# First MoE: the two halves of a tile's transposes set apart, with the next tile's last product piece and its exponential between them

## The chip, the cores and the metric

The program runs on one core of one Trainium2 chip. The metric is the device time of one execution in microseconds; before the change the median of three runs is 1106.28 us.

## The reference

Three stages follow one another. Attention: for 4 batches and 8 heads of 576 tokens and head size 64, scores q·kᵀ/8 plus a position bias from a small two-layer network, softmax, times v. Its output, seen as 2304 tokens of 512 values, is the input of the first MoE block; the output of that is the input of the second. The change is in the first block:

```
h = x @ w_in                                # 2304 x 512 by 512 x 1024
e = exp(h - max(h));  sm = e / (sum(e) + 1e-9)
solu = h * sm
ln = (solu - mean) / sqrt(var + 1e-6) * g_ln
x2 = ln @ w_out                             # 1024 x 512
```

The second block is `(sigmoid(x2 @ w_gate) * (x2 @ w_val)) @ w_out2`, with a width of 1536.

## The kernel before, in words

**Number format.** Every fp32 operand of a product is cut into a high and a low fp16 part, and a product is three fp16 products (high·high, high·low, low·high) summed in PSUM.

**Attention** runs in 72 ticks. In tick t TensorE does the scores of tick t (`a_qk`, s_ps, L500), the products with v of tick t-4 (`a_pv`, xps, L560) and, in some ticks, transposes of finished outputs (`a_xt`, xtp, L606), of q (`prep_q`, qtp, L276) and of k (`prep_k`, ktp, L237). VectorE adds the bias and takes the row maximum (L520), ScalarE takes the exponentials (L525, L527), ScalarE or VectorE and then GpSimd cut the result into fp16 parts (L536 to L540), and a DMA on SP's queue transposes them (pt).

**First MoE.** There are 18 tiles of 128 tokens. For one tile i the steps, in the code's terms, are: `m_g1`, the first product in four pieces, two (half 0, half 1) for each of two column halves n = 0, 1, of 6 matmuls of 512 columns each (L702, into hps); after half 1 of each n VectorE copies the accumulator out and takes its maximum (L713). `m_ew1`: the exponential on ScalarE (e, L723) and the product with h on VectorE (L727). `m_ew2`: squares on ScalarE (L733), the power on GpSimd, then the normalisation on GpSimd (L738). `m_ew3`: the layer transposes, two halves of four fp32 transposes each (ltp, L747); each half is copied out as the fp16 high part by ScalarE (lt, L749), and VectorE subtracts for the low part (L750). `m_g2`: the second product in four pieces dc of 24 small matmuls (x2ps, L761); a piece reads all eight 128-column blocks of lt, the four of the first half first. With dc = 3 the result is copied out (L766, L767) and stored (x2_d, L769).

**What sets the order.** A generator, `moe_items`, lists these steps. For each i it gives the four pieces of `m_g1(i)`, then `m_ew1(i)`, then `m_ew3(i-1)` with both halves, then `m_ew2(i)`, then the four pieces of `m_g2(i-1)`: eleven items a tile. From the moment the bias work is over, each tick takes three items (NB = 3), after `a_qk` and ahead of `a_pv` and `a_xt`. The transposes of q and k that a tick brings come right behind the first of the three items. A tile's first piece has to wait for its tokens, so that some ticks take no item. In the attention stage TensorE's order is the written one (`manual_schedule`); that of the other engines is made by the planner, from priorities and modelled times, attention ahead of MoE. hps, ltp, x2ps, qtp, ktp and xtp share three PSUM buffers (`ps_m`); hps of one n holds its buffer from half 0 until VectorE has copied it out after half 1.

When the ticks are over, the items that are left (from the last piece of tile 14 on) are issued in one go, and between them the preparation of the second MoE's weights (loads wraw, L630; decoding on ScalarE and VectorE, w2f, L168 to L173). There the planner orders TensorE too, and each time a tile's result is stored ten units of weight work are queued behind that store. In this stage `m_g1` takes its accumulators from a pair in another pool (`glob["tail"]`, s_ps).

Of the kernel before, what the change touches and what calls it, by code (L numbers as in the profile page):

```python
# [8 lines left out]
F32 = mybir.dt.float32  # L9
F16 = mybir.dt.float16  # L10
BF16 = mybir.dt.bfloat16
I32 = mybir.dt.int32
ACTF = mybir.ActivationFunctionType
ALU = mybir.AluOpType
# [57 lines left out]
LAG_PV = 4  # L72
LAG_X = 1
# [15 lines left out]
def attn_moe_kernel(  # L89
# [7 lines left out]
    act, dve, pool, pe, sp = nc.scalar, nc.vector, nc.gpsimd, nc.tensor, nc.sync  # L97
    AX = mybir.AxisListType.X

    def enter(stack, name, bufs=1, side="left", space=None):  # L100
        kw = {} if space is None else {"space": space}
        if space is None:
            kw["reuse_waits"] = "tile"
            kw["side"] = side
        return stack.enter_context(tc.tile_pool(name=name, bufs=bufs, **kw))
# [13 lines left out]
    ps_m = enter(pss, "ps_m", 3, space=PSUM)  # L119
# [3 lines left out]
    id_sb = const.tile([128, 128], F32, name="id_sb")  # L123
# [558 lines left out]
    mo = {}  # L682

    def tile_x(i):
        t = tiles[i]
        if t[0] == "M":
            return XT[t[1], "M"], 0
        _, bp, qd, b, r = t
        return XT[bp, qd, b], 128 * r

    def m_g1(i, n, half):
        xt, off = tile_x(i)
        if half == 0 and "tail" in glob:
            if n == 0:
                glob["tail"] = ps_s.tile([128, 2, 512], F32, name="s_ps", tag="s_ps")
            mo[i, "h", n] = glob["tail"][:, n]
        elif half == 0:
            mo[i, "h", n] = ps_m.tile([128, 512], F32, name="hps", tag="m")
        h = mo[i, "h", n]
        for kk in (0, 1) if half == 0 else (2, 3):  # L700
            for (xl, wl) in ((0, 0), (0, 1), (1, 0)):
                pe.matmul(  # L702
                    h, xt[:, xl, kk, off:off + 128], win16[:, 2 * kk + n, wl],
                    start=(kk == 0 and xl == 0 and wl == 0), stop=(kk == 3 and xl == 1),
                )
        if half == 0:
            return
        if n == 1:
            done.add(("g1", i))
        if n == 0:  # L710
            mo[i, "m"] = glob["ms"].tile([128, 16], F32, name="mm")
            mo[i, "hs"] = glob["hs"].tile([128, FF1], F32, name="hs")
        dve.tensor_tensor_reduce(out=mo[i, "hs"][:, 512 * n:512 * n + 512], in0=mo.pop((i, "h", n)),  # L713
                                 in1=zero.to_broadcast([128, 512]), scale=1.0, scalar=-3.0e38,
                                 op0=ALU.add, op1=ALU.max, accum_out=mo[i, "m"][:, 11 + n:12 + n])

    def m_ew1(i):
        m, hs = mo[i, "m"], mo[i, "hs"]
        e = glob["e"].tile([128, FF1], F32, name="e")
        mo[i, "e"] = e  # L720
        dve.tensor_scalar(out=m[:, 1:2], in0=m[:, 11:12], scalar1=m[:, 12:13], scalar2=col(NC1),
                          op0=ALU.max, op1=ALU.mult)
        act.activation(out=e, in_=hs, func=ACTF.Exp, bias=m[:, 1:2], scale=col(C1), accum_out=m[:, 2:3])  # L723
        dve.tensor_scalar(out=m[:, 3:4], in0=m[:, 2:3], scalar1=1e-9, scalar2=None, op0=ALU.add)
        dve.reciprocal(m[:, 3:4], m[:, 3:4])
        dve.tensor_scalar(out=m[:, 3:4], in0=m[:, 3:4], scalar1=col(C1), scalar2=None, op0=ALU.mult)
        dve.scalar_tensor_tensor(out=e, in0=hs, scalar=m[:, 3:4], in1=e, op0=ALU.mult, op1=ALU.mult,  # L727
                                 accum_out=m[:, 4:5])
        dve.tensor_scalar(out=m[:, 5:6], in0=m[:, 4:5], scalar1=-1.0 / FF1, scalar2=None, op0=ALU.mult)

    def m_ew2(i):
        m, e = mo[i, "m"], mo[i, "e"]
        act.activation(out=mo.pop((i, "hs")), in_=e, func=ACTF.Square, bias=m[:, 5:6], accum_out=m[:, 6:7])  # L733
        dve.tensor_scalar(out=m[:, 7:8], in0=m[:, 6:7], scalar1=1.0 / FF1, scalar2=1e-6, op0=ALU.mult, op1=ALU.add)
        pool.tensor_tensor(out=m[:, 8:9], in0=m[:, 7:8], in1=nhalf, op=ALU.pow)
        dve.tensor_scalar(out=m[:, 9:10], in0=m[:, 8:9], scalar1=512.0, scalar2=None, op0=ALU.mult)
        dve.tensor_scalar(out=m[:, 10:11], in0=m[:, 9:10], scalar1=m[:, 5:6], scalar2=None, op0=ALU.mult)
        pool.tensor_scalar(out=e, in0=e, scalar1=m[:, 9:10], scalar2=m[:, 10:11], op0=ALU.mult, op1=ALU.add)  # L738

    def m_ew3(i):  # L740
        mo.pop((i, "m"))
        e = mo.pop((i, "e"))
        lt = glob["lt"].tile([128, 2, 8, 128], F16, name="lt")
        for n in range(2):
            tp = ps_m.tile([128, 4, 128], F32, name="ltp", tag="m")
            for f in range(4):
                pe.transpose(tp[:, f], e[:, 512 * n + 128 * f:512 * n + 128 * f + 128], id_sb)  # L747
            hi = lt[:, 0, 4 * n:4 * n + 4]
            act.activation(out=hi, in_=tp, func=ACTF.Copy)  # L749
            dve.tensor_tensor(out=lt[:, 1, 4 * n:4 * n + 4], in0=tp, in1=hi, op=ALU.subtract)  # L750
        mo[i, "lt"] = lt

    def m_g2(i, dc):
        lt = mo[i, "lt"]
        if dc == 0:
            mo[i, "x2"] = ps_m.tile([128, 4, 128], F32, name="x2ps", tag="m")
        ps = mo[i, "x2"]
        n = 0
        for f in range(8):
            for (wl, ll) in ((0, 0), (0, 1), (1, 0)):  # L760
                pe.matmul(ps[:, dc], wout16[:, f, wl, 128 * dc:128 * dc + 128], lt[:, ll, f],  # L761
                          start=(n == 0), stop=(n == 23))
                n += 1
        if dc == 3:
            x2 = glob["x2"].tile([128, 4, 2, 128], F16, name="x2")
            act.activation(out=x2[:, :, 0], in_=ps, func=ACTF.Copy, scale=2.0 ** -15)  # L766
            dve.scalar_tensor_tensor(out=x2[:, :, 1], in0=ps, scalar=2.0 ** -15, in1=x2[:, :, 0],  # L767
                                     op0=ALU.mult, op1=ALU.subtract)
            glob["st"] = sp.dma_start(out=x2_d[i], in_=x2)  # L769
            mo.pop((i, "lt"))  # L770
            mo.pop((i, "x2"))


    ticks, tiles, ready = [], [], []
# [42 lines left out]
    for n, (bb, hp) in enumerate(order):  # L817
        t0 = used[bb, hp]
        for nm, src, prep, lag in (("k", k, prep_k, 0), ("v", v, prep_v, LAG_PV)):
            if (bb, hp) == (0, 0):  # L820
                continue
            f = freed[order[n - 8]] + lag + 1 if n >= 8 else 4 * (n // 2 - 1) if n >= 4 else 0
# [3 lines left out]
            when(u, lambda bb=bb, hp=hp, prep=prep: prep(bb, hp), at if nm == "v" else late)  # L826

    def moe_items():
        for i in range(19):
            if i < 18:  # L830
                for n in range(2):
                    for half in range(2):
                        yield ready[i] + LAG_PV + LAG_X + 1, (lambda i=i, n=n, half=half: m_g1(i, n, half))
                yield 0, (lambda i=i: m_ew1(i))
            if i >= 1:
                yield 0, (lambda i=i: m_ew3(i - 1))
            if i < 18:
                yield 0, (lambda i=i: m_ew2(i))
            if i >= 1:
                for dc in range(4):  # L840
                    yield 0, (lambda i=i, dc=dc: m_g2(i - 1, dc))
# [97 lines left out]
    glob = {}  # L939
# [15 lines left out]
    def side_work():  # L955
        bq = []
        for t in (4, 2, 3):
            bq += list(bias_tile(t))
            bq += [lambda t=t: done.add(("bias", t))]
        wq = list(w1_steps())  # L960
        while wq:
            for _ in range(NWB):
                if wq:
                    yield 0, wq.pop(0)
            yield 0, bq.pop(0)
        yield 0, s1.close
        for f in bq:
            yield 0, f
        yield 0, open_moe
        yield from moe_items()  # L970
# [367 lines left out]
    for g in range(1, 5):  # L1338
        n = 4 if g < 4 else 2
# [81 lines left out]
```

## Time and profile before

| | us |
|---|---|
| runs | 1100.22, 1106.28, 1108.24 (median 1106.28) |
| the profiled execution | 1103.77 |
| its span, first to last instruction | 1102.0 |

| engine | busy us in the span | share |
|---|---|---|
| TensorE (PE) | 911.8 | 83% |
| VectorE (DVE) | 811.1 | 74% |
| ScalarE (ACT) | 627.5 | 57% |
| GpSimd (POOL) | 426.4 | 39% |

The profile is of one execution. An engine's busy time is the time in which it executes instructions; PE's is modelled, since matmuls overlap. The row named PEclk is the share of TensorE's full clock that was granted. In rows of a timeline a bracket says how long the engine was idle ahead of the row and what ended that. All times count from the first instruction.

### The profile page before, as it was taken

Reading aid. Unit: us, or ns where it says so; the run is one execution under the profiler, and the core shown is the slowest. Engines: PE = TensorE matmul, PEld = TensorE weight load, DVE = VectorE, ACT = ScalarE, POOL = GpSimd, SP = SyncE. Lnnn points to the kernel's source line nnn. Section 1 sums busy time; section 2 is a strip of 40 time slices with the busy share of each in tenths; the row PEclk is TensorE's granted clock in tenths of the full one; section 3 lists DMA queues with packets and bytes.
Section 4 is the critical chain, followed back from the end, with each engine's and each line's share of the span. In section 5 each row is a group of like instructions: output and inputs, shape, how many; then the busy total and the mean of one; then the engine's idle time right before and its main releaser. Section 6 shows DMA issues by size and latency. Waiting matters only on the chain.

```text
span 1102.0 us, 24792 instructions
## 1 busy us (share of the span) xinstructions
PE 911.8 (83%) x9950; PEld 641.8 (58%) x9950; DVE 811.1 (74%) x1647; ACT 627.5 (57%) x1302; POOL 426.4 (39%) x365
## 2 busy tenths in 40 slices
PE   2554774678778889889999778798999899999998
PEld 2442553456456666767776456343477488488585
DVE  6797999897557776666774889989949568257453
ACT  4858567766567788877883667654323233123232
POOL 2566366473455466545552266749000000000000
PEclk9655666657898999999999899998999999999999
DMA  9948899698979899999957536621000100100000
GB/s 281 306 136 294 179 201 216 132 185 187 211 144 191 183 194 196 185 198 202 211 110 173 163 106 188 188 75 38 20 21 2 66 10 1 48 11 1 20 21 20
DMA packets 259715, 146.41 MB, mean 133 GB/s; under 512 B 216976, under 2 KB 229648, under 8 KB 259600
## 3 DMA queue, kind: packets, MB, share of 16 engines
q1 hardware_dynamic: 258064, 143.25, 55.1%
q0 software_dynamic: 1536, 1.58, 0.5%
q8 instruction: 78, 1.28, 0.5%
q14 instruction: 37, 0.30, 0.1%
HBM read 82.27 MB, written 20.05 MB: 93 GB/s over the span
## 4 chain that ended last, share of the span: by engine, by line
PE 29%; DVE 13%; issue 3%; ACT 2%; DMA 2%; POOL 1%; SPq 0%; POOLq 0%; DVEq 0%; ACTq 0%
PE prod L1229 14%; PE ops L1297 10%; DVE fr L1153 2%; DVE w2f L170 2%; DVE fs L1153 2%; DVE w2f L173 2%; PE x2ps L761 2%; DMA wraw<-in_moe_w_val_dram 1%; DVE gv L1135 1%; PE hps L702 1%; DMA wraw<-in_moe_w_gate_dram 1%; DVE w2f L169 1%; DVE w2s L1153 1%; PE xps L560 1%; DVE fr L1273 1%
## 5 line engine op out<-in xcount | busy, mean ns | idle before, releaser
L539 POOL TENSOR_TENSOR p<-p,p 128x1024 f16<-128x1024 f32 x72 | 154.5, 2146 | 154.3 <-ACT p L538 105.3
L1153 DVE TENSOR_TENSOR fr<-prod,fr 128x512 f32<-128x512 f32 (+1 forms) x154 | 91.8, 614 | 108.1 <-PE prod L1229 104.1
L1297 PE MATMUL ops<-w2f,gv 128*128 128x512 f16 x648 | 144.4, 382 | 4.3 <-DVE gv L1135 3.1
L527 ACT ACTIVATE p<-p,m,sc 128x576 f32<-128x576 f32 x144 | 124.0, 862 | 2.8
L761 PE MATMUL x2ps<-lt,w1f 128*128 128x128 f16 x1728 | 106.5, 221 | 12.7 <-DVE lt L750 11.9
L761 PEld LDWEIGHTS <-w1f 128*128 128x128 f16 x1728 | 100.7, 99 | 22.6 <-issue 18.8
L520 DVE CUSTOM_DVE_ANT_0 p<-s_ps,gk 128x576 f32<-128x576 f32 x144 | 104.2, 751 | 11.7 <-PE s_ps L500 8.6
L1297 PEld LDWEIGHTS <-gv 128*128 128x128 f16 x648 | 63.4, 98 | 79.6 <-DVE gv L1135 3.6
L1267 PE MATMUL s_ps<-xb,w2f 128*128 128x512 f16 x384 | 90.3, 392 | 18.0 <-DVE fr L1273 13.2
L409 PEld LDWEIGHTS <-mask 128*128 128x128 f16 (+1 forms) x1312 | 64.9, 122 | 65.8 <-issue 28.7
L500 PE MATMUL s_ps<-gk,qt 64*128 64x288 f16 (+1 forms) x960 | 94.8, 323 | 9.4 <-DVE m L520 5.4
L1229 PEld LDWEIGHTS <-w2f 128*128 128x128 f16 x1056 | 92.2, 98 | 11.7 <-issue 1.4
L560 PE MATMUL xps<-gk,pt 128*128 128x64 f16 (+1 forms) x2240 | 87.8, 202 | 12.1 <-DMA pt<-p 12.1
L560 PEld LDWEIGHTS <-pt 128*128 128x128 f16 (+1 forms) x2240 | 81.7, 107 | 25.2 <-DMA pt<-p 13.9
L702 PE MATMUL hps<-w1f,xt 128*128 128x512 f16 x312 | 77.9, 401 | 0.6 <-DVE qt L279 0.6
L409 PE MATMUL bp<-rhs,mask 128*128 128x64 f16 (+1 forms) x960 | 53.8, 227 | 29.2 <-DVE gb L434 14.8
L1267 PEld LDWEIGHTS <-w2f 128*128 128x128 f16 x384 | 38.2, 100 | 66.9 <-issue 26.0
L1134 ACT ACTIVATE gv<-fr 128x512 f16<-128x512 f32 (+1 forms) x60 | 34.7, 586 | 70.9 <-DVE fr L1287 65.7
L1229 PEld LDWEIGHTS <-w2s 128*128 128x128 f16 x792 | 69.2, 98 | 7.4 <-issue 0.3
L538 ACT ACTIVATE p<-p 128x1152 f16<-128x1152 f32 x54 | 62.6, 1159 | 14.1 <-DMA pt<-p 12.4
L525 ACT ACTIVATE m<-m,sc 128x1 f32<-128x1 f32 x144 | 40.5, 286 | 48.1 <-DVE m L520 48.0
L702 PEld LDWEIGHTS <-xt 128*128 128x128 f16 x384 | 37.2, 102 | 50.4 <-issue 16.4
(196 smaller groups left out, 1852.9 us busy)
## 6 DMA issues: line engine op xcount, KB each, us to landing
gk<-bias_d SPq DMA_DIRECT2D x24, 576.0 KB, 4.8
wraw<-in_moe_w_out_dram SPq DMA_DIRECT2D x20, 512.0 KB, 4.3
wraw<-in_moe_w_gate_dram SPq DMA_DIRECT2D x12, 512.0 KB, 4.1
wraw<-in_moe_w_val_dram SPq DMA_DIRECT2D x12, 512.0 KB, 3.8
sraw<-in_q_dram SPq DMA_DIRECT2D x12, 384.0 KB, 5.5
sraw<-in_k_dram SPq DMA_DIRECT2D x12, 384.0 KB, 3.8
sraw<-in_v_dram SPq DMA_DIRECT2D x12, 384.0 KB, 4.2
bias_d<-gk SPq DMA_DIRECT2D x8, 576.0 KB, 8.8
```

The source lines that it names most:

```text
L409: pe.matmul(big[0:np_, jj // 8, o:o + 64], lhsT, rhs[i].rearrange("p c h g -> p (c h g)"), start=(i == 0), stop=(i == 1),)
L500: pe.matmul(ss[hh][p0:p1, n, 0:288], qt[rows, nr * ql + r, p0:p1], kt[rows, o:o + 288], start=(m == 0), stop=(m == 2))
L520: dve.tensor_tensor_reduce(out=pp[:, hh].rearrange("p (i j) -> p i j", i=2), in0=ss[hh][:, :, 0:288], in1=bi.rearrange("p (i j) -> p i j", ...
L527: act.activation(out=pp[:, hh], in_=pp[:, hh], func=ACTF.Exp, bias=m[:, 2 + hh:3 + hh], scale=col(C), accum_out=sm[:, c + hh:c + hh + 1])
L539: pool.tensor_tensor(out=p16[:, :, 640:1152], in0=pp[:, :, 0:512], in1=hi[:, :, 0:512], op=ALU.subtract)
L560: pe.matmul(o, a, b_, start=(n == 0), stop=(n == len(seq) - 1))
L702: pe.matmul(h, xt[:, xl, kk, off:off + 128], win16[:, 2 * kk + n, wl], start=(kk == 0 and xl == 0 and wl == 0), stop=(kk == 3 and xl == 1),)
L761: pe.matmul(ps[:, dc], wout16[:, f, wl, 128 * dc:128 * dc + 128], lt[:, ll, f], start=(n == 0), stop=(n == 23))
L1153: dve.tensor_tensor(out=out_, in0=a, in1=b, op=op)
L1229: pe.matmul(p[:, jf, 0:nn], w(wl, kk, jf), x(xl, kk), start=(m == 0), stop=(m == 5))
L1267: pe.matmul(ps[:, 0:n], w[:, 4 * (j // 4) + c, wl, o:o + 128], xx[:, 0:n, c, xl, :], start=(m == 0), stop=(m == 11))
L1297: pe.matmul(ps, gvs[j // 4][:, gl, j % 4, 128 * tt:128 * tt + 128], w2h16[2][:, j, wl], start=(m == 0), stop=(m == 35))
```

## The change

`m_ew3` takes the half as an argument and does one half per call; lt is allocated with the first half. In `moe_items` the first half of tile i-1 comes ahead of the last piece of `m_g1(i)`, and the second half behind `m_ew1(i)`. A tile now has twelve items in place of eleven. Where the last stage's accumulators are chosen, a test is added for the case that its pair isn't there yet.

```diff
-        if half == 0 and "tail" in glob:
+        if half == 0 and "tail" in glob and (n == 0 or glob["tail"] is not None):
...
-    def m_ew3(i):
-        mo.pop((i, "m"))
-        e = mo.pop((i, "e"))
-        lt = glob["lt"].tile([128, 2, 8, 128], F16, name="lt")
-        for n in range(2):
-            tp = ps_m.tile([128, 4, 128], F32, name="ltp", tag="m")
-            for f in range(4):
-                pe.transpose(tp[:, f], e[:, 512 * n + 128 * f:512 * n + 128 * f + 128], id_sb)
-            hi = lt[:, 0, 4 * n:4 * n + 4]
-            act.activation(out=hi, in_=tp, func=ACTF.Copy)
-            dve.tensor_tensor(out=lt[:, 1, 4 * n:4 * n + 4], in0=tp, in1=hi, op=ALU.subtract)
-        mo[i, "lt"] = lt
+    def m_ew3(i, n):
+        e = mo[i, "e"]
+        if n == 0:
+            mo.pop((i, "m"))
+            mo[i, "lt"] = glob["lt"].tile([128, 2, 8, 128], F16, name="lt")
+        lt = mo[i, "lt"]
+        tp = ps_m.tile([128, 4, 128], F32, name="ltp", tag="m")
+        for f in range(4):
+            pe.transpose(tp[:, f], e[:, 512 * n + 128 * f:512 * n + 128 * f + 128], id_sb)
+        hi = lt[:, 0, 4 * n:4 * n + 4]
+        act.activation(out=hi, in_=tp, func=ACTF.Copy)
+        dve.tensor_tensor(out=lt[:, 1, 4 * n:4 * n + 4], in0=tp, in1=hi, op=ALU.subtract)
+        if n == 1:
+            mo.pop((i, "e"))
...
     def moe_items():
+        def g1(i, n, half):
+            return ready[i] + LAG_PV + LAG_X + 1, lambda: m_g1(i, n, half)
+
         for i in range(19):
             if i < 18:
-                for n in range(2):
-                    for half in range(2):
-                        yield ready[i] + LAG_PV + LAG_X + 1, (lambda i=i, n=n, half=half: m_g1(i, n, half))
+                yield g1(i, 0, 0)
+                yield g1(i, 0, 1)
+                yield g1(i, 1, 0)
+            if i >= 1:
+                yield 0, (lambda i=i: m_ew3(i - 1, 0))
+            if i < 18:
+                yield g1(i, 1, 1)
                 yield 0, (lambda i=i: m_ew1(i))
             if i >= 1:
-                yield 0, (lambda i=i: m_ew3(i - 1))
+                yield 0, (lambda i=i: m_ew3(i - 1, 1))
             if i < 18:
                 yield 0, (lambda i=i: m_ew2(i))
```

## Rows read from the trace of the kernel before

**Rows 1.** The page: TensorE's granted clock in 40 slices of the span, in tenths.

```profile
PEclk9655666657898999999999899998999999999999
```

**Rows 2.** Windows: PE, PEld, DVE, ACT, POOL busy us (instructions), PEclk, DMA.

```profile
271.00:400.00 129.00, 104.82 (x1363) 74.46 (x1358) 82.32 (x205) 89.19 (x197) 70.70 (x68) 0.91 0.89 182
400.00:600.00 200.00, 185.29 (x2884) 140.48 (x2881) 133.30 (x365) 156.30 (x347) 107.87 (x88) 1.00 0.93 180
600.00:700.00 100.00, 82.63 (x737) 53.30 (x737) 88.78 (x196) 66.70 (x137) 53.04 (x46) 0.95 0.54 174
```

**Rows 3.** Waits of PE, 285 to 600 us: total us, times, longest.

```profile
PE x2ps L761 <- DVE lt L750: 10.4, 9, 2.5
PE ltp L747 <- DVE mm L713: 3.8, 4, 2.0
PE ktp L237 <- DVE mm L713: 3.8, 2, 2.0
...
PE ltp L747 <- DVE gk L240: 2.6, 3, 1.5
...
PE ltp L747 <- DVE qt L279: 0.7, 1, 0.7
```

**Rows 4.** Timeline of PE: start, us; then the same engine a little earlier.

```profile
458.59 1.09 PE L747 MATMUL ltp<-id_sb,e 128*128 128x128 f32 x8
459.52 0.27 PE L276 MATMUL qtp<-id_sb,qraw 128*128 128x128 f32 x1
462.31 1.39 PE L761 MATMUL x2ps<-lt,w1f 128*128 128x128 f16 x22 [2.52 <-DVE lt L750]
...
448.07 1.51 PE L761 MATMUL x2ps<-lt,w1f 128*128 128x128 f16 x24
449.42 2.75 PE L702 MATMUL hps<-w1f,xt 128*128 128x512 f16 x12
```

**Rows 5.** Timeline of ACT over the same stretch.

```profile
459.72 1.24 ACT L723 ACTIVATE e<-hs,mm,sc 128x1024 f32<-128x1024 f32 x1 [1.53 <-DVE mm L721]
...
460.96 0.57 ACT L749 ACTIVATE lt<-ltp 128x512 f16<-128x512 f32 x1
```

**Rows 6.** Timeline of DVE over the same stretch.

```profile
461.56 0.69 DVE L750 TENSOR_TENSOR lt<-ltp,lt 128x512 f16<-128x512 f32 x1 [0.33 <-ACT lt L749]
...
463.22 1.27 DVE L727 SCALAR_TENSOR_TENSOR e<-hs,mm,e 128x1024 f32<-128x1024 f32 x1
```

**Rows 7.** Timeline of PE at two other tiles of the same layout.

```profile
546.30 1.46 PE L702 MATMUL hps<-w1f,xt 128*128 128x512 f16 x6
...
549.35 1.09 PE L747 MATMUL ltp<-id_sb,e 128*128 128x128 f32 x8
...
552.55 1.50 PE L761 MATMUL x2ps<-lt,w1f 128*128 128x128 f16 x24 [1.89 <-DVE lt L750]
...
359.40 1.09 PE L747 MATMUL ltp<-id_sb,e 128*128 128x128 f32 x8
...
362.49 1.50 PE L761 MATMUL x2ps<-lt,w1f 128*128 128x128 f16 x24 [0.32 <-DVE lt L750]
```

**Rows 8.** Timeline of PE at transposes of k.

```profile
291.91 0.37 PE L237 MATMUL ktp<-id_sb,kv 64*128 64x64 f32 x1 [3.18 <-DVE mm L729]
292.21 5.30 PE L702 MATMUL hps<-w1f,xt 128*128 128x512 f16 x12
...
353.50 0.36 PE L237 MATMUL ktp<-id_sb,kv 64*128 64x64 f32 x1 [3.15 <-DVE qt L279]
```

**Rows 9.** Timeline of PE, then POOL: one tile's last piece, and its normalisation.

```profile
505.39 1.47 PE L702 MATMUL hps<-w1f,xt 128*128 128x512 f16 x6
...
522.38 1.20 POOL L738 TENSOR_SCALAR e<-e,mm 128x1024 f32<-128x1024 f32 x1
```

**Rows 10.** Timeline of SP's queue: a result's store and the next weight loads.

```profile
599.20 0.32 SPq L769 DMA_DIRECT2D x_d<-x  x1
599.57 7.41 SPq L630 DMA_DIRECT2D wraw<-in_moe_w_gate_dram  x4
```

## The prediction, made before the changed kernel was run

> **What bounds the kernel now.** I read the clock of the page and the windows first, to see which engine paces the stage in which the moved steps lie; then TensorE's waits there; then timelines of single tiles, to see what a wait is made of. The change touches only the first MoE, which runs inside the attention ticks until about 600 us and after them until some 690. Between 400 and 600 us PE is busy for 185.29 of 200 us at a clock of 1.00, and the next engine, ScalarE, for 156.30; between 271 and 400 us PE has 104.82 of 129 us, at 0.91, still ahead of the others [rows 2]. The clock dips within that stretch and is full later [rows 1]. PE's order is written there, so it either works or stands at one instruction while everything behind it stands too: a microsecond of waiting taken from PE is nearly a microsecond of the stage. The views of waits give what can be had: 10.4 us in 9 waits of the second product for a layer copy, 3.8 + 2.6 + 0.7 = 7.1 us in waits of the transposes for a PSUM buffer, and more at the transposes of k [rows 3]. From 600 us VectorE leads with 88.78 of 100 us [rows 2], decoding weights.
>
> **The order that results.** Counting items, three to a tick, a tile of twelve takes exactly four ticks: [three pieces of the first product], [first transposes, fourth piece, exponential], [second transposes, squares, first piece of the second product], [its other three pieces]. With eleven items this pattern drifted, and only in three of the 13 tiles before the stage's end did the second product follow the transposes within a tick. Now it does so in every one of the 13. The stage still ends with three pieces of tile 14 issued, so the work on either side of that border is the same, and the added test in `m_g1` never decides: the first pair that the last stage asks for is that of tile 15, with n = 0. No instruction, DMA or byte is added or removed; SP's and GpSimd's queues get the same entries.
>
> **Part 1, the transposes' waits go.** The first half now comes while VectorE has had a tick to empty hps of n = 0; the second comes a tick later, behind `a_pv` and `a_qk`, when the buffer of n = 1 is being emptied. Of the 7.1 us I leave 1 for that race: -6.1 us, bounds -7.1 and -3. The normalised e must be there earlier, too. In one of the slow tiles its last piece starts at 505.39 and GpSimd ends at 522.38 + 1.20 = 523.58 [rows 9], some 16.9 us after that piece ends. Two last pieces, two tiles apart, start at 505.39 and 546.30 [rows 7, 9]: 20.5 us a tile, and the first half now stands one piece and itself ahead of the next last piece, 1.3 + 0.5 us. That leaves 18.7, so 1.8 us of cover; nothing is charged.
>
> **Part 2, the second product waits more often.** The cost is in three tiles that already have the new neighbourhood. At 458.59 eight transposes ran, then one of q, then the second product stood 2.52 us until 462.31 [rows 4]. ScalarE shows why: it had the next tile's exponential (459.72, 1.24 us) ahead of the layer copy, which began at 460.96 [rows 5], and VectorE's subtraction from 461.56 took 0.69 [rows 6]. In the changed order the first half is long copied, but the second half stands behind the exponential in just this way. So I keep the moment of release, 462.31, and move PE: four transposes end at 458.59 + 0.47 = 459.06; one of q adds 0.27; the twelve matmuls on the first half can run at once, 12 × 0.056 = 0.67 us (24 of them take 449.42 - 448.07 = 1.35) [rows 4]. PE is then at 460.0 and waits 2.3. At 549.35 the same reckoning gives 552.55 - 550.76 = 1.8; at 359.40, where transposes of k lie between and the wait was for the second of two subtractions, 362.49 - 0.69 - 360.54 = 1.3 [rows 6, 7]. The mean is 1.8 us, and I take it, as it comes from the nearest rows: 13 × 1.8 = 23.4 in place of 10.4, **+13.0 us**. The lower bound is a copy that starts at once, 0.57 + 0.69 + 0.06 to PE's start = 1.32 [rows 4 to 6], less the cover of 0.94: 0.4 us a tile. The upper bound lets the product of the exponential on VectorE, 1.27 us [rows 6], go first as well: 3.1 us.
>
> **Part 3, the transposes of k.** In eight ticks of tiles 1 to 4 q's and k's transposes come behind the tick's first item. Where that item has just begun an accumulator, its buffer can't be freed, and two are left: such ticks cost 3.18 us (291.91) and 3.15 (353.50) [rows 8], others 3.8 in two [rows 3]. Now all four first ticks of those tiles begin so, two more than before (+1.3 us each); in the second ticks k meets a first half of ltp and an accumulator begun the tick before, which may cost nothing, or the 0.96 to 1.3 of a copy. Against this, k's wait behind both layer copies goes, and longer waits of PE swallow some waits for loads. I take +1, bounds -5 and +10.
>
> **Part 4, after 600 us.** There the planner sets PE's order as well. The first weight load left SP's queue at 599.57, right behind the store of tile 12 at 599.20 [rows 10], so that a later tile 12 delays the weights and the stage's shift is passed on, not lost. Tile 12's store comes in the last ticks behind one more `a_pv`, and tile 13's first half comes a piece earlier: 0, bounds -4 and +4.
>
> **The sum**: 1103.77 - 6.1 + 13.0 + 1 + 0 = 1111.7, so **1112 us**. It is made against the profiled execution, which is 2.5 us below the median of 1106.28 and inside the runs' 1100 to 1108; I leave that as uncertainty.
>
> **Rivals.** *The copy goes first.* If the planner puts the second half's copy ahead of the exponential on ScalarE, PE waits 0.4 us a tile: 13 × 0.4 - 10.4 = -5.2, and the sum is 1093.5. For it: ScalarE stood idle 1.53 us ahead of the exponential [rows 5], time in which the copy was ready. Against it: in the rows of the same layout it let that time pass, and the code lists the exponential ahead of the second half. It decides from a wait of 0.5 us a tile down (1095.2 - 1103.8 = -8.6 = -6.1 + 1 + 13w - 10.4).
> *The product goes first too.* With 3.1 us a tile the term is +29.9 and the time 1128.6. It decides from 2.2 us a tile up. For it: one of the three rows gives 2.3 by itself. Against it: the subtractions went ahead of the product there [rows 6].
> *The end swallows it.* Weight decoding, not PE, may set the end whatever tile 12 does; then 1103 to 1107. For it VectorE's 88.78 [rows 2], against it SP's order [rows 10].
> [...]
>
> **How the numbers follow.** About 1% is what a measurement of this kernel can tell from no change: 1095.2 to 1117.3. The forecast's case has 0.50, with 0.09 of it above 1117.3; the copy first 0.16 (0.12 of it below 1095.2); the product first 0.18 (0.17 above); the end swallows it 0.14, all within; the clock 0.02. That makes faster 0.12, slower 0.28, within 0.60. The range reaches to the middle of the copy-first and the product-first cases, 1093 to 1129, which leaves about 0.08 + 0.11 outside.
>
> **What would show it.** Waits of PE from 285 to 600 us: ltp's should nearly vanish, and the second product's for lt should be near 23 us in 13 waits, each behind twelve matmuls, with ScalarE's exponential just ahead of the second copy. k's transposes should wait in four first ticks for about 3 us. The first weight load should leave some 8 us later than 599.57. The prediction is wrong if the second product's waits sum to less than 15.5 us (-6.1 + 1 - 10.4 + 15.5 = 0), or if the load is later and the end is not.

## The result, and the profile after

Three runs of the changed kernel take 1117.93 us in the median (1116.71 to 1125.59) against 1106.28 before: the ratio is 1.0148, with a 95% interval of 1.0108 to 1.0188. It is slower, as forecast, by about twice the forecast's step against that median: 1112 was predicted, inside a range that reaches to 1129. The profiled execution took 1116.71 us, 12.9 more than the one before, where the sum, which was made against that one, had 7.9.

TensorE's waits in the same window as [rows 3]; columns: total us, times, longest.

```profile
PE x2ps L763 <- DVE lt L751: 10.9, 10, 1.6
PE ktp L237 <- DVE qt L279: 8.0, 3, 2.7
PE ktp L237 <- DVE lt L751: 7.9, 4, 2.4
PE x2ps L763 <- ACT lt L750: 7.7, 6, 1.4
PE x2ps L763 <- DVE xtm L624: 3.9, 1, 3.9
PE ktp L237 <- DVE mm L729: 3.2, 1, 3.2
...
```

The waits of the layer transposes (7.1 us in [rows 3]) are gone to the last one. Those of the second product are 10.9 + 7.7 = 18.6 for a layer copy and 3.9 for a PSUM buffer, 22.5 in place of 10.4, and those of k's transposes 21.2 (with 1.9 and 0.2 that are not shown) in place of 15.4. All waits of PE in the window sum to 45.5 us after and 36.6 before: 8.9 us more. The changed kernel's stage ends later than this window, but up to 613 us only one more wait comes, of 0.4 us.

One tile on PE, start and us; the first four transposes are the second half's. This answers to [rows 4].

```profile
443.24 0.66 PE L748 MATMUL ltp<-id_sb,e 128*128 128x128 f32 x4
443.74 0.38 PE L276 MATMUL qtp<-id_sb,qraw 128*128 128x128 f32 x2
443.95 0.83 PE L763 MATMUL x2ps<-lt,w1f 128*128 128x128 f16 x12
446.04 0.22 PE L763 MATMUL x2ps<-lt,w1f 128*128 128x128 f16 x1 [1.25 <-ACT lt L750]
447.29 0.89 PE L763 MATMUL x2ps<-lt,w1f 128*128 128x128 f16 x11 [1.04 <-DVE lt L751]
447.98 1.70 PE L560 MATMUL xps<-gk,pt 128*128 128x64 f16 x28
449.61 1.62 PE L500 MATMUL s_ps<-gk,qt 64*128 64x288 f16 x12
```

Twelve matmuls run on the first half, then PE stands for the high part of the second half, does one matmul, and stands again for its low part: 2.3 us. The same stretch on ScalarE:

```profile
443.13 1.23 ACT L723 ACTIVATE e<-hs,mm,sc 128x1024 f32<-128x1024 f32 x1
...
444.36 1.15 ACT L538 ACTIVATE p<-p 128x1152 f16<-128x1152 f32 x1
445.41 0.57 ACT L750 ACTIVATE lt<-ltp 128x512 f16<-128x512 f32 x1
```

The copy has both the exponential and attention's cut of p ahead of it. And on VectorE:

```profile
445.34 1.28 DVE L727 SCALAR_TENSOR_TENSOR e<-hs,mm,e 128x1024 f32<-128x1024 f32 x1
...
446.55 0.69 DVE L751 TENSOR_TENSOR lt<-ltp,lt 128x512 f16<-128x512 f32 x1
```

The product with h goes ahead of the subtraction, which it did not in [rows 6]. In six of the tiles 4 to 10 the wait is 1.8 to 2.4 us, in tiles 0 to 3 0.8 to 1.6, in tiles 11 and 12 at most 0.4. Tile 8 is another case: there PE stands 3.9 us ahead of the first matmul of the piece, for a PSUM buffer in which transposes of attention's output still lie. Their copy on VectorE (xtm, L624) stood behind the product with h, which took 2.58 us in this tile.

The last two rows of PE's fence show the second loss: right behind the waits 28 matmuls with v took 1.70 us and 12 score matmuls 1.62, where 0.98 and 0.91 are usual. The windows show the lower clock at such moments; first the stretch of [rows 2], then a short window in it (PE busy us and instructions, PEclk, DMA).

```profile
400.00:600.00 200.00, 180.67 (x2660) 136.19 (x2658) 125.03 (x341) 149.83 (x332) 108.48 (x85) 0.95 0.86 169
```

```profile
448.00:452.00 4.00, 4.00 (x57) 0.60 1.16 183
```

Before, no such window of 4 us between 400 and 600 us is below 1.00; after, seven are below 0.9. Five of them lie behind a wait of the second product, in tiles 4, 5, 6, 8 and 10; the two others, side by side at 404, lie behind waits of the scores.

On SP's queue, the rows that answer to [rows 10]:

```profile
600.28 13.97 SPq L630 DMA_DIRECT2D wraw<-in_moe_w_gate_dram  x3
614.33 0.40 SPq L771 DMA_DIRECT2D x_d<-x  x1
```

Tile 12's store is at 614.33, 15.1 us later than in [rows 10]. The first weight load is only 0.7 us later: the planner put three loads ahead of that store. But the second of them had to wait 8.7 us for attention's last normalised output (xn, L593), so the queue stood anyway. The decoding of the 36 weight blocks then runs at its old pace: the first block's last step on VectorE starts at 618.5 in place of 605.9, the last block's at 741.2 in place of 729.0. The shift at the end of attention is the shift of the whole.

### The profile page after: what moved, and what is told of

It reads as the page before. It is cut to its first block, busy times and chain, and to the rows that moved or that the text cites. A ratio compares the mean times of both kernels' runs of the same rounds, so it can differ in the third digit from the quotient of the medians.

```text
span 1114.9 us, 24780 instructions
## 1 busy us (share of the span) xinstructions
PE 922.6 (83%) x9950; PEld 649.8 (58%) x9950; DVE 806.2 (72%) x1647; ACT 628.5 (56%) x1302; POOL 428.5 (38%) x365
## 4 chain that ended last, share of the span: by engine, by line
PE 32%; DVE 14%; issue 3%; ACT 2%; DMA 2%; POOL 1%; SPq 0%; DVEq 0%; POOLq 0%; ACTq 0%
PE prod L1238 14%; PE ops L1306 10%; PE x2ps L763 3%; DVE fr L1162 2%; PE hps L702 2%; DVE w2f L170 2%; DVE fs L1162 2%; DVE w2f L173 1%; PE xps L560 1%; DMA wraw<-in_moe_w_val_dram 1%; DVE gv L1144 1%; PE s_ps L500 1%; DVE w2f L169 1%; DVE e L727 1%; DVE w2s L1162 1%
## 5 line engine op out<-in xcount | busy, mean ns | idle before, releaser
L539 POOL TENSOR_TENSOR p<-p,p 128x1024 f16<-128x1024 f32 x72 | 159.4, 2214 | 161.3 <-ACT p L538 85.4
L763 PE MATMUL x2ps<-lt,w1f 128*128 128x128 f16 x1728 | 112.8, 224 | 24.8 <-DVE lt L751 13.0
L763 PEld LDWEIGHTS <-w1f 128*128 128x128 f16 x1728 | 104.6, 100 | 35.1 <-issue 32.6
L560 PE MATMUL xps<-gk,pt 128*128 128x64 f16 (+1 forms) x2240 | 90.0, 204 | 10.5 <-DMA pt<-p 10.3
L500 PEld LDWEIGHTS <-qt 64*128 64x128 f16 (+1 forms) x960 | 48.9, 108 | 34.2 <-issue 14.7
L538 ACT ACTIVATE p<-p 128x1152 f16<-128x1152 f32 x54 | 62.5, 1157 | 10.6 <-DMA pt<-p 8.9
```

Of the source, the lines that this page charges most:

```text
L500: pe.matmul(ss[hh][p0:p1, n, 0:288], qt[rows, nr * ql + r, p0:p1], kt[rows, o:o + 288], start=(m == 0), stop=(m == 2))
L539: pool.tensor_tensor(out=p16[:, :, 640:1152], in0=pp[:, :, 0:512], in1=hi[:, :, 0:512], op=ALU.subtract)
L560: pe.matmul(o, a, b_, start=(n == 0), stop=(n == len(seq) - 1))
```

## Experiments

Two theories went into the first four. A: the loss is the second product's wait for the second half's copy, and the slow clock behind it. B: the loss is the four-tick layout of twelve items. Each ratio is to the kernel before, run on the same chip. The changed kernel was not run again beside them: a step from its 1117.93 us lies between two chips, and by the ratios it can come out some 3 us otherwise.

**The exponential behind the copy.**

```diff
-                yield 0, (lambda i=i: m_ew1(i))
-            if i >= 1:
-                yield 0, (lambda i=i: m_ew3(i - 1, 1))
+                yield 0, (lambda i=i: None if i else m_ew1(0))
+
+            def late(i=i):
+                if i >= 1:
+                    m_ew3(i - 1, 1)
+                if 1 <= i < 14:
+                    with tc.issue_after(glob["cp"].ins):
+                        m_ew1(i)
...
+            if i:
+                yield 0, late
```

(in the changed kernel; `glob["cp"]` is the second half's copy on ScalarE)

> TensorE's order of the changed kernel is kept instruction for instruction up to the end of the attention stage; only ScalarE is told to take the next tile's exponential behind the copy of the second half (tiles 1 to 13), so that the product on VectorE comes behind the subtraction too. Theory A (the loss is the second product's wait for the second half, queued behind exponential, attention's split and product, and the slow clock behind that wait): the waits of the second product for lt fall from 23 us to 5 to 12, the granted clock from 404 to 503 us goes back from 0.93 towards 1.00, and the time is 1100 to 1108 us, ratio to before 0.995 to 1.002. Theory B (the loss is the new spread of twelve items over four ticks, whatever ScalarE's order): time as the changed kernel, 1115 to 1120, ratio 1.010 to 1.015.

Measured: 1109.85 us, ratio 1.0044 (1.0019 to 1.0068). PE's waits, and the window from 404 us:

```profile
PE qtp L276 <- DMA qraw<-in_q_dram: 6.6, 2, 4.2
PE x2ps L763 <- DVE lt L751: 6.1, 9, 1.0
...
PE x2ps L763 <- ACT lt L750: 1.4, 5, 0.4
```

```profile
404.00:503.00 99.00, 87.34 (x1339) 67.27 (x1336) 65.36 (x181) 81.23 (x186) 54.17 (x47) 0.97 0.95 186
```

With PE's order unchanged, one edge on ScalarE takes the second product's waits for lt from 18.6 (10.9 + 7.7) to 7.5 us, the clock of this window from 0.93 to 0.97, and 8 us off the median (the product with h on VectorE follows the exponential). That is theory A's main cause shown, in the size of the wait, but the time stayed 2 us above what A had expected. Part was given back: q's transposes now wait 6.6 us for loads that came in time for the slower kernel. And 22 us of waits at k's transposes remain.

**The second half ahead of the exponential.** The first half keeps its new place.

```diff
                 yield g1(i, 1, 1)
-                yield 0, (lambda i=i: m_ew1(i))
             if i >= 1:
                 yield 0, (lambda i=i: m_ew3(i - 1, 1))
             if i < 18:
+                yield 0, (lambda i=i: m_ew1(i))
                 yield 0, (lambda i=i: m_ew2(i))
```

(in the changed kernel)

> Of the change only the first half's place is kept: it stays ahead of the next tile's last piece, and the second half goes right behind that piece, ahead of the exponential. Still twelve items in four ticks. Theory A: both copies are done a_pv and a_qk before the second product starts, its waits for lt nearly vanish (under 4 us in 13 tiles), some of the transposes' waits for a buffer come back (up to 7 us), time 1094 to 1104, ratio 0.988 to 0.998. Theory B: 1113 to 1119, since the items a tick and the transposes of k stand as in the changed kernel.

Measured: 1107.79 us, ratio 1.0036 (1.0009 to 1.0064).

```profile
PE ktp L237 <- DVE lt L751: 8.0, 4, 2.4
PE ktp L237 <- DVE qt L279: 6.8, 3, 2.3
PE qtp L276 <- DMA qraw<-in_q_dram: 6.4, 2, 4.0
```

The second product's waits for lt are gone altogether, as A said, and yet the time is 4 us above A's range: k's transposes still wait, and q's wait for loads. What is left here is what A lacks.

**The old order in twelve items.**

```diff
-            if i >= 1:
-                yield 0, (lambda i=i: m_ew3(i - 1, 0))
-            if i < 18:
                 yield g1(i, 1, 1)
                 yield 0, (lambda i=i: m_ew1(i))
             if i >= 1:
-                yield 0, (lambda i=i: m_ew3(i - 1, 1))
+                yield 0, (lambda i=i: (m_ew3(i - 1, 0), m_ew3(i - 1, 1)))
             if i < 18:
                 yield 0, (lambda i=i: m_ew2(i))
+            if i >= 1:
+                yield 0, (lambda: None)
```

(in the changed kernel)

> The order of the kernel before, both halves together behind the exponential, with one empty item behind the squares, so that a tile has twelve items and takes four ticks as in the changed kernel; the second product's four pieces then fall one tick behind the squares. Theory A: the transposes stand last in a tick, a_pv and a_qk hide most of the copies, second-product waits 5 to 12 us and transposes' waits for a buffer up to 8, time 1102 to 1110, ratio 0.996 to 1.004. Theory B: the four-tick layout alone costs, 1112 to 1119.

Measured: 1111.6 us, ratio 1.0066 (1.0046 to 1.0086).

```profile
PE x2ps L763 <- DVE lt L751: 10.7, 11, 2.2
PE ktp L237 <- DVE qt L279: 8.3, 3, 2.8
...
PE ltp L748 <- DVE gk L240: 3.4, 4, 0.9
PE ltp L748 <- DVE mm L713: 3.3, 6, 1.0
```

It lies between the two expectations. The layout of four ticks by itself costs some 6.6 us: so B holds for a part, and neither theory alone. PE's waits sum to 40.6 us where they were 36.6; the growth is in q's waits for loads (4.3 for 1.6), in the second product's (12.1 for 10.4) and in the scores' (2.3 for 0.6). k's transposes wait 13.8, not more than before, and the clock from 400 to 600 us is 1.00. What the rest of the 6.6 us is stays open.

**Both halves first.** Eleven items.

```diff
             if i >= 1:
-                yield 0, (lambda i=i: m_ew3(i - 1, 0))
+                yield 0, (lambda i=i: (m_ew3(i - 1, 0), m_ew3(i - 1, 1)))
             if i < 18:
                 yield g1(i, 1, 1)
                 yield 0, (lambda i=i: m_ew1(i))
-            if i >= 1:
-                yield 0, (lambda i=i: m_ew3(i - 1, 1))
-            if i < 18:
                 yield 0, (lambda i=i: m_ew2(i))
```

(in the changed kernel)

> Both halves together at the first half's new place, ahead of the next tile's last piece and its exponential; eleven items a tile as before. Theory A: copies lie well ahead of the exponential and of the second product, waits for lt under 5 us, but two halves meet an accumulator that is being filled, so that the second half waits for the first one's copy (1 to 2 us in each of 13 tiles): time 1098 to 1110, ratio 0.992 to 1.004. Theory B: eleven items drift as before, 1104 to 1108, ratio 0.998 to 1.002.

Measured: 1098.52 us, ratio 0.994 (0.9916 to 0.9963). The waits of the second product for lt vanish, as A said, the second half's wait for the first one's copy hardly shows, and k's transposes wait 13.6 us. New is a wait of q's transposes for a buffer that a copy still holds:

```profile
PE qtp L276 <- DVE lt L751: 8.9, 4, 3.7
```

So it was not wrong to bring the transposes ahead of the last piece. What was wrong is that one half was held back, or that this made a twelfth item, or both: this run undoes both at once, and no run has both halves first in twelve items.

**The wait filled with work.**

```diff
         for f in range(8):
+            if dc == 0 and f == 4 and i < 13:
+                for _ in range(30):
+                    pe.matmul(ps[:, 3], wout16[:, 0, 0, 0:128], lt[:, 0, 0], start=False, stop=False)
```

(in the changed kernel)

> The changed kernel, with 30 extra small matmuls (1.7 us at the full clock) put between the twelve matmuls on the first half and the rest of the second product's first piece, in tiles 0 to 12: the place where TensorE otherwise waits 2.3 us. They write columns that a later piece overwrites. The copy's release is not moved. If the slow clock that follows the wait carries part of the loss, the granted clock from 404 to 503 us rises from 0.93 to 0.98 or more and the time falls by 4 to 9 us against the changed kernel, to 1109 to 1114, though 390 matmuls are added. If the wait alone carries it, the time stays or rises, 1117 to 1124.

Measured: 1135.26 us, ratio 1.0288 (1.0248 to 1.0329): a miss of both expectations. One tile on PE, a wait further on, and the window:

```profile
452.28 0.83 PE L766 MATMUL x2ps<-lt,w1f 128*128 128x128 f16 x12
452.95 1.84 PE L764 MATMUL x2ps<-lt,w1f 128*128 128x128 f16 x30
...
455.62 0.78 PE L766 MATMUL x2ps<-lt,w1f 128*128 128x128 f16 x11 [0.77 <-DVE lt L751]
456.23 0.98 PE L560 MATMUL xps<-gk,pt 128*128 128x64 f16 x28
...
502.19 0.66 PE L276 MATMUL qtp<-id_sb,qraw 128*128 128x128 f32 x2 [5.00 <-DVE e L727]
502.64 1.49 PE L766 MATMUL x2ps<-lt,w1f 128*128 128x128 f16 x12
503.92 3.05 PE L764 MATMUL x2ps<-lt,w1f 128*128 128x128 f16 x30
```

```profile
404.00:503.00 99.00, 88.83 (x1409) 69.32 (x1406) 67.20 (x181) 77.91 (x177) 57.01 (x44) 0.98 0.97 178
```

In this tile the filler stands where the wait was, the 28 matmuls behind it take 0.98 us again, and the window's clock is 0.98 for 0.93. The same holds in tiles 4, 6, 9 and 10. From 404 us on the clock falls twice, each time behind a wait that is not filled: 5.00 us of q's transposes, and tile 8's 3.90 us ahead of its first matmul; the filler itself then takes 3.05 and 2.96 us in place of 1.84. The time rose all the same: the filler is 390 × 0.056 = 21.8 us, the second product's waits only fell from 22.5 to 8.0, the wait of 5.00 us is new, and from 265 to 404 us the clock was 0.89, where the changed kernel had 0.94. The clock stays up where the wait is filled (0.98 for 0.93); what that would give by itself, this run can't say.

**q's and k's transposes behind a tick's second item.**

```diff
             side_step(t)
-            if n == 0:
+            if n == (1 if "s" in glob else 0):
```

(in the changed kernel, in the order with both halves first, and in the kernel before)

> The changed kernel, with the transposes of q and k of a tick behind its second MoE item and not behind the first, so that the accumulator begun by the first item is complete when they ask for a buffer. If the held accumulator is what the transposes of k wait for, their 21 us fall to 14 or less and the time falls by 5 to 10 us, to 1108 to 1113; q's transposes then lie ahead of the second product less often, which may cost it 1 to 3 us. If those waits hang on the copies and not on the accumulator, they stay at 18 to 24 us and the time at 1115 to 1120.

Measured: 1110.87 us, ratio 1.0055 (1.0027 to 1.0084).

```profile
PE x2ps L763 <- ACT lt L750: 11.2, 9, 1.5
PE x2ps L763 <- DVE lt L751: 7.0, 10, 1.0
...
PE ktp L237 <- DVE lt L751: 1.0, 2, 0.6
```

k's transposes wait 9.5 us in place of 21.2, those for lt 1.0 in place of 7.9, and 7 us come off the median. The accumulator that a tick's first item begins, together with the first half beside it, was what they waited for. Part of the wait moved: the first product now waits 5.8 us for copies of q's and k's transposes, where it waited for none. The second product's waits for lt are untouched, 18.2 us.

> The order with both halves ahead of the next tile's last piece (eleven items), and with q's and k's transposes behind a tick's second item. By the held accumulator they wait less than the 20 us that they wait for in that order, and the time falls from 1098.5 to 1092 to 1097, ratio to before 0.985 to 0.993. If their waits only move to another place, 1097 to 1102, ratio 0.993 to 0.998.

Measured: 1093.95 us, ratio 0.9913 (0.9885 to 0.994): faster than both kernels, by 10.6 us than the one before. One tile on PE:

```profile
449.00 1.04 PE L748 MATMUL ltp<-id_sb,e 128*128 128x128 f32 x8
449.88 1.46 PE L702 MATMUL hps<-w1f,xt 128*128 128x512 f16 x6
451.17 0.98 PE L560 MATMUL xps<-gk,pt 128*128 128x64 f16 x28
452.09 0.91 PE L500 MATMUL s_ps<-gk,qt 64*128 64x288 f16 x12
452.93 0.33 PE L276 MATMUL qtp<-id_sb,qraw 128*128 128x128 f32 x1
453.09 1.50 PE L763 MATMUL x2ps<-lt,w1f 128*128 128x128 f16 x24
```

Between the eight transposes and the second product stand some 3 us of other work, and no row has a wait. But the reason expected for the further 4.6 us is not borne out: q's and k's transposes together wait 10.3 + 9.6 = 19.9 us here and 8.9 + 13.6 = 22.5 in the order without this edit, and all waits of PE from 285 us to the stage's end sum to 30.9 us against 28.7. The clock from 265 to 404 us is 0.94 against 0.91, and the intervals of the two ratios overlap. Where the 4.6 us come from, and whether they are more than the difference between two sets of executions, stays open.

> The kernel before, with the transposes of q and k of a tick behind its second MoE item and not behind the first: this edit by itself. If it is what made the version with both halves first faster by another 4.6 us, it gives 1097 to 1102 here, ratio 0.993 to 0.998. If it helps only where an accumulator is begun by a tick's first item, which the old drifting order does in few ticks, 1103 to 1108, ratio 0.998 to 1.003.

Measured: 1103.2 us, ratio 0.9992 (0.9969 to 1.0016): no difference, as the second expectation said. The edit is worth 7 us beside the changed order and nothing beside the old one.

**The changed order after the ticks only, and in the first ticks only.** In these two the place of the halves depends on i; the second has `i < 5` in the first line.

```diff
+            new = i >= 14
...
-            if i >= 1:
+            if i >= 1 and new:
                 yield 0, (lambda i=i: m_ew3(i - 1, 0))
...
-                yield 0, (lambda i=i: m_ew3(i - 1, 1))
+                yield 0, (lambda i=i, new=new: (None if new else m_ew3(i - 1, 0), m_ew3(i - 1, 1)))
```

(in the changed kernel)

> The changed order for the steps of i = 14 and later only, that is after the attention ticks; until then the order of the kernel before. If the loss lies in the attention stage, as the waits say, this is 1102 to 1109 us, ratio 0.997 to 1.003. If the planner's new order after the ticks costs, 1109 to 1114, ratio 1.004 to 1.008.

Measured: 1104.38 us, ratio 1.0003 (0.9977 to 1.0028). After the ticks the change shows no cost, to within 3 us.

> The changed order up to the steps of i = 4 (about 270 to 390 us), from there the order of the kernel before. If the loss is spread as TensorE's time by stretch says (137.4 to 139.7 us until tick 40, 93.0 to 98.2 until tick 57, 99.9 to 110.1 until tile 12's end), only some 2 to 5 us of it are here: 1106 to 1111, ratio 1.001 to 1.006. If the transposes of k, which are in this stretch alone, are the heart of the loss, 1112 to 1118, ratio 1.006 to 1.013.

Measured: 1113.13 us, ratio 1.008 (1.0048 to 1.0111): above what the stretches had said, and inside the second expectation. k's transposes wait 20.2 us here too, and the clock is another than in the changed kernel:

```profile
265.00:404.00 139.00, 112.43 (x1441) 77.45 (x1437) 84.07 (x217) 95.09 (x211) 71.20 (x69) 0.89 0.88 180
```

The changed kernel ran this stretch, in which PE's order is the same, at 0.94. So the clock here differs by 5 points between two programs with the same order, and the parts of the loss can't be told by adding stretches to better than some 139 × 0.05 = 7 us. Nor does the run place its loss in the first ticks. PE's waits from 285 to 610 us sum to 38.1 us, 1.5 more than those of the kernel before in its window; in the profiled execution, the slowest of its seven, tile 12's store (605.74) is 6.5 us later than before and the end 13.0, so that half of the excess comes where the order is that of the kernel before. How much of this run's 9 us belongs to k's transposes stays open.

## Why the prediction was right, and where its sum was short

**The transposes' waits (part 1)**: -6.1 forecast, all 7.1 us went. Right.

**The second product's waits (part 2)**: 23.4 us forecast, 22.5 measured, of which 18.6 for lt, behind twelve or thirteen matmuls each, with the exponential ahead of the copy; 3.9 are tile 8's wait for a PSUM buffer, which was not in the forecast. Right in mechanism, and the run with the exponential behind the copy shows it as cause. That the size came out is in part luck. The chain was longer than the rows I took it from: in tiles 4 to 10 attention's cut went ahead of the copy too, and in five of them (4, 5, 6, 9, 10) the product with h ahead of the subtraction, 2.3 to 2.4 us a tile. (One of my three rows, 549.35, has two transposes of q behind it, 0.38 us, where I reckoned one: 1.7 and not 1.8, which does not move the mean.) The rival with the product first came true there; the first four tiles and the last two, which waited less, and tile 8's other wait brought the sum back to the forecast.

**k's transposes (part 3)**: this term was mis-sized: +1 forecast, 15.4 to 21.2, so +5.8 measured, inside the bounds. I had named the state (a first half of ltp and an accumulator begun) and let a gain elsewhere cancel it. The wait for lt alone is 7.9 us in four times; it is there in each run with one half ahead of k's transposes (7.6 to 8.2), and 1.0 where they come a piece later. The four ticks alone do not make it: with both halves together in twelve items k's transposes wait 13.8.

**After 600 us (part 4)**: 0 forecast; with the change there alone 1.0003. The reason I gave for the shift being passed on was wrong: not tile 12's store but the end of attention holds SP's queue. The sign that I had named, a first weight load some 8 us later, did not come: it was 0.7 us later. The step came out because the end of attention and tile 12's store move together.

**The clock, the term that failed.** I gave a fall of TensorE's clock behind the waits 0.02 and left it out of the sum, since one wait of 2.52 us had been followed by 22 matmuls in 1.39 us, the usual pace of 24 in 1.51 [rows 4]. The trace before says otherwise of a longer wait (twelve matmuls in 5.30 us behind 3.18, [rows 8]), and it had a row that says otherwise for short waits, and I passed over it: after 2.00 and 0.64 us, with one transpose between them, twelve matmuls took 4.44 us where 2.75 is usual.

```profile
323.73 0.27 PE L237 MATMUL ktp<-id_sb,kv 64*128 64x64 f32 x1 [2.00 <-DVE mm L713]
324.64 4.44 PE L702 MATMUL hps<-w1f,xt 128*128 128x512 f16 x12 [0.64 <-DVE qt L279]
```

In the changed kernel some of the waits were followed by slow matmuls: of the six of 1.8 to 2.4 us in tiles 4 to 10, four had 28 matmuls with v in 1.42 to 1.70 us right behind them (tiles 4, 5, 6 and 10) and two the usual 0.98 (tiles 7 and 9). The clock was 0.95 from 400 to 600 us where it had been 1.00. Of the programs above that have the old order there, the one with the change after the ticks only has 0.99 and the one with the change in the first ticks only 0.97. So the clock of this stretch differs between programs with one order, too, and part of the fall may be that; but where the waits were filled with matmuls the clock stayed up, 0.98 from 404 to 503 us for 0.93. What makes the clock fall behind one wait and not behind another is not shown.

With the waits' +8.9 the stage would end at 608; tile 12's store is at 614.33. Those last 6 us are the size of the slow stretches: the clock after was 0.94, 0.93 and 0.97 in stretches of 139, 99 and 110 us, before 0.91, 1.00 and 1.00 in the same work, and 99 × 0.07 + 110 × 0.03 - 139 × 0.03 = 6.1 us. No run took the clock away with all else equal, and the first stretch alone spreads by 7 us, so this is an estimate, not shown.

**The layout** was not in the sum: twelve items in four ticks cost some 6.6 us even in the old order. Part of what I booked as waits may be this: the edit at the exponential gives 8 us back and the one at k's transposes 7, which with the layout is more than the whole loss of 11.65, so the parts overlap and can't be added.

## What to carry to other kernels

Where the copies that a consumer waits for are on an engine whose order is set in advance, ask what of the next round stands ahead of the last copy, not of the first. Where a tick takes a fixed number of items, one more item per round moves every other step against the tick, and that alone can cost as much as the wait that was to be removed (here some 6.6 us, beside 7.1). And a wait that is put into each round of a stretch at full clock can cost more than its length, if the trace shows slow matmuls behind any wait at all: here two waits of 2.3 us together had 28 matmuls behind them in 1.70 us, where 0.98 is usual.

## What the runs showed of the hardware that was not expected

A pair of waits of 1.25 and 1.04 us with one matmul between them was followed by a clock of 0.60 from 448 to 452 us (446.04, 447.29: 28 matmuls in 1.70 us), while the same pair in another tile of the same execution was not:

```profile
543.54 0.22 PE L763 MATMUL x2ps<-lt,w1f 128*128 128x128 f16 x1 [1.25 <-ACT lt L750]
544.80 0.77 PE L763 MATMUL x2ps<-lt,w1f 128*128 128x128 f16 x11 [1.04 <-DVE lt L751]
545.41 0.98 PE L560 MATMUL xps<-gk,pt 128*128 128x64 f16 x28
```

Nor was the single wait of 2.52 in [rows 4], with 22 matmuls in 1.39 us behind it. In these rows the length of a wait alone does not tell whether the clock falls behind it.
